# Right-hand steps of the first down layer placed beside the first half of each row pair only, one block of the weight combinations kept in another buffer, one warm-up matmul less

## The chip, the cores and the metric

The kernel runs on one core of one Trainium2 chip. The metric is the device time of one execution in microseconds (us), as the median of several runs. The kernel before took 1056.25 us (three runs, 1054.87 to 1056.70).

## The reference

The program is one attention layer with a sigmoid in place of the softmax, followed by two feed-forward blocks, all in float32:

```
scores = q @ k.T / sqrt(64) - log(448);  attn = sigmoid(scores);  x = attn @ v      (4 batches, 12 heads, 448 x 64)
xn = x / rms(x) * rms_g;   y = (silu(xn @ w_gate) * (xn @ w_val)) @ w_out             (1792 tokens, 768 -> 1536 -> 768)
h  = ((y @ w1) * (y @ w2)) @ w3;   out = h @ w_out2                                    (768 -> 1024 -> 1024 -> 768)
```

The kernel multiplies w3 by w_out2 first, so the second block ends with one product of h's 1024 features by a combined 1024 x 768 matrix. That product is called the down layer here.

## The kernel before, in words

Everything is computed transposed: features on the 128 partitions, 448 tokens (one batch) along the free axis. A product of float32 accuracy is made of three matmuls of a split number (high part by high part, low by high, high by low; `runs`, L339 to L347). Most layers use a Winograd form of the two-by-two block product: seven products of combined blocks in place of eight. The left-hand combinations (of the weights) are made by `Weights.winograd_blocks` (L164 to L183), the right-hand ones (of the activations) by `right_steps` (L569 to L638).

The four batches are worked in two pairs. For pair 0, then for pair 1, the last part of the program is an up layer (`c_winograd`, eight row blocks) and the down layer (`d_winograd`, L692 to L713, three row pairs n = 0, 1, 2). The first down layer is the one of pair 0. Each of its row pairs consists of two halves (e = 2n and e = 2n + 1), each half of seven parts, each part of six matmuls of 448 columns, which accumulate in the PSUM bank of that part: four banks of the tag `w` and three of the tag `m` (`psm`). In the second half the seven products come out one after the other, and `combine` (L715 to L745) takes each from PSUM: ScalarE copies product 0 to u (L721), and VectorE adds the others: product 1 to v (L724), then L728, L731, L734, two of L738 and L739, and L743. Until VectorE (or ScalarE) has read a bank, TensorE can't begin the same part of the next row pair.

Beside it runs a list of generators, `todo`; each call of `step` (L660) advances the first of them by one piece. In the first down layer they are: what is left of the combinations of the last h block (five steps); and for k = 0, 1, 2 `y_steps(k)` (L667), which prepare the right-hand blocks of the second pair's up layer. A `y_steps(k)` loads four tiles `ys` from DRAM (first step; the buffers of the tag `held` are four, so each load waits until the tile that had the buffer is no longer read), does nothing for one step, and begins with its third: two subtractions t1 and t2 from `ys` (the second needs the fourth tile) and the first of seven `put`s. A put lets ScalarE copy the high part, and VectorE subtract it for the low part in the step after (`low`, L587). A `y_steps` takes ten steps; the one of k = 2 takes `wait` more, since its last four puts go to buffers that the down layer itself reads until its last row pair. All these VectorE instructions have line L575 and are pinned behind the instruction that was traced before them on VectorE (`keep_in_program_order`); the others are ordered by the planner, which simulates the program with estimated costs and issues an engine's ready instruction that was traced first.

The weights come as four quarters a11, a12, a21, a22 in one tile `wd`; `winograd_blocks` makes two sums and a difference (L171 to L173), yields six blocks, and makes the seventh, a12 - s2, at L179. Each yielded block is copied for its high part by ScalarE (L134), and GpSimd subtracts that for the low part (L138). L179 writes the seventh over a12, which was the third block.

At the start, eight matmuls of a tile of ones (L81 and L82, `WARM`) run on TensorE while the first inputs arrive; each is two matmul instructions in the trace.

Of the kernel before, what the change touches and what calls it, by code (L numbers as in the profile page):

```python
# [13 lines left out]
ALU = mybir.AluOpType  # L14
# [19 lines left out]
AHEAD_B1 = (2, 2, 2, 0, 0, 0)  # L34
AHEAD_B2 = (2, 2, 2, 1, 1, 0)
WH = 3 * P
WARM = 8
STEP = 8


# [5 lines left out]
def fused_kernel(ctx: ExitStack, tc: tile.TileContext, qkv, wg, wv, wo, w1, w2, w3, wo2, gam, out):  # L46
    nc = tc.nc
# [32 lines left out]

    for _ in range(WARM):  # L81
        nc.tensor.matmul(ps_m.tile([P, 512], F32, tag="m", bufs=3, name="psm")[:, :P], ones, ones, start=True, stop=True)  # L82
# [5 lines left out]
    def scratch(name):  # L88
        return scr.tile([P, S], F32, tag="s", bufs=6, name=name)
# [4 lines left out]
    def psm():  # L94
        return ps_m.tile([P, 512], F32, tag="m", bufs=3, name="psm")
# [44 lines left out]
    class Weights:  # L140
# [23 lines left out]
        def winograd_blocks(self):  # L164

            while True:
                f, w, keep = self.loaded.pop(0)
                a11, a12, a21, a22 = (f[:, j, k * w : (k + 1) * w] for j in range(2) for k in range(2))
                s = wp.tile([P, WT], F32, tag="mag", bufs=1, name="s")
                s1, s2 = s[:, :w], s[:, w : 2 * w]  # L170
                nc.vector.tensor_tensor(out=s1, in0=a21, in1=a22, op=ALU.add)  # L171
                nc.vector.tensor_tensor(out=s2, in0=s1, in1=a11, op=ALU.subtract)  # L172
                nc.vector.tensor_tensor(out=a21, in0=a11, in1=a21, op=ALU.subtract)  # L173
                if keep is not None:
                    nc.sync.dma_start(out=keep[0], in_=s2)
                    nc.sync.dma_start(out=keep[1], in_=a21)
                    nc.sync.dma_start(out=keep[2], in_=s1)
                yield from (a11, s2, a12, a21, a22, s1)
                nc.vector.tensor_tensor(out=a12, in0=a12, in1=s2, op=ALU.subtract)  # L179
                if keep is not None:  # L180
                    nc.sync.dma_start(out=keep[3], in_=a12)
                self.out -= 1
                yield a12  # L183

        def make_blocks(self):

# [152 lines left out]
    def runs(ps, wtile, kw, xts, first, last):  # L339

        n = len(xts)
        for r, (wi, xi) in enumerate(RUNS):
            for j, xt in enumerate(xts):
                w = wtile[:, wi, (kw + j) * P : (kw + j + 1) * P]
                nc.tensor.matmul(  # L345
                    ps, w, xt[:, xi, :], start=first and r == 0 and j == 0, stop=last and r == 2 and j == n - 1
                )  # L347
# [211 lines left out]
    def right_tile(name, bl):  # L559
        p, n, step = {0: (r1a, 6, STEP), 1: (r1b, 6, 0), 2: (pools["xw"], 9, STEP)}[bl]  # L560
        return parts(p, f"x{bl}", n, name, step=step)

    def ab_tile(name, n):

        if n < 2 * KF1:
            return h_tile(name, n // 2)
        return right_tile(name, (n - 2 * KF1) // 2)

    def right_steps(k, b, home=None, down=False, wait=None):  # L569

        def sub(out, in0, in1, op=ALU.subtract):
            i = nc.vector.tensor_tensor(out=out, in0=in0, in1=in1, op=op)  # L575
            if down or wait is not None:
                tc.keep_in_program_order(i)

        late = []

        def put(j, bl, src):
            t = acts["d" if down else "w", j, k] = ab_tile(f"w{j}", 7 * k + j) if down else right_tile(f"w{j}", bl)
            nc.scalar.activation(t[:, 0, :], src, AF.Copy)
            low()
            late.append((t, src))

        def low():  # L587
            if late:
                t, src = late.pop()
                sub(t[:, 1, :], src, t[:, 0, :])  # L590

        if wait is None:
            put(0, 0, b[0])
            yield
            t1 = home()
            sub(t1, b[1], b[0])
            put(5, 1, t1)
            yield
            while len(b) < 4:
                low()  # L600
                yield
            put(2, 0, b[2])
            yield
            t3 = home()
            sub(t3, b[3], b[1])
            put(3, 2, t3)
            yield
            t2 = home()
            sub(t2, t3, b[0], ALU.add)
            put(1, 2, t2)  # L610
            yield
            t4 = home()
            sub(t4, b[2], t2)
            put(4, 2, t4)
            yield
            put(6, 1, b[3])
            yield
            low()
            return
        t1 = scratch("t1")  # L620
        sub(t1, b[1], b[0])
        t2 = scratch("t2")
        sub(t2, b[3], t1)
        put(1, 2, t2)
        yield
        sub(b[1], b[3], b[1])
        put(3, 2, b[1])
        yield
        sub(t2, b[2], t2)
        put(4, 2, t2)  # L630
        yield
        for _ in range(wait):
            low()
            yield
        for j, bl, x in ((0, 0, b[0]), (2, 0, b[2]), (5, 1, t1), (6, 1, b[3])):
            put(j, bl, x)
            yield
        low()  # L638
# [7 lines left out]
    def load_y(g, k):  # L646
        y = []
        for m in (k, k + 3):
            for b in range(2):
                y.append(held("ys"))  # L650
                nc.sync.dma_start(out=y[-1], in_=yd.pop((g, b, m)))
        return y
# [7 lines left out]
    def step():  # L660

        if todo:
            next(todo[0], None)
            if inspect.getgeneratorstate(todo[0]) == inspect.GEN_CLOSED:
                todo.pop(0)

    def y_steps(k):  # L667
        y = load_y(1, k)
        for _ in range(2):
            yield  # L670
        yield from right_steps(k, y, wait=5 if k == 2 else 0)

    def product_bank():
        return psm()[:, :S]
# [1 line left out]
    def bank():  # L676
        return ps_w.tile([P, 512], F32, tag="w", bufs=4, name="w")[:, :S]
# [14 lines left out]
    def d_winograd(g, first, n):  # L692

        ps = [bank() if j < 4 else psm()[:, :S] for j in range(7)]

        def part(e, j):
            i, c = divmod(7 * e + j, 3)
            t = W.get(first + i)[:, :, c * 2 * P : (c + 1) * 2 * P]
            h = D_HALVES[e][1]
            runs(ps[j], t, 0, [acts["d", j, 2 * h + k] for k in range(2)], e == 2 * n, e > 2 * n)  # L700
            W.split_to(first + i + 3)
            W.load_to(first + i + 6)
            return ps[j]

        def done(b, *rows):
            for j, o in enumerate(rows):
                m = 2 * n + j
                nc.sync.dma_start(out=out[m * P : (m + 1) * P, (2 * g + b) * S : (2 * g + b + 1) * S], in_=o)

        for j in range(7):  # L710
            part(2 * n, j)
            step()
        combine(lambda j: part(2 * n + 1, j), done)  # L713

    def combine(product, done, home=None):  # L715

        tt = nc.vector.tensor_tensor

        u, v, c21 = (scratch(n) for n in ("u", "v", "c21"))
        p1 = product(0)  # L720
        nc.scalar.activation(u, p1, AF.Copy)  # L721
        step()
        p6 = product(1)
        tt(out=v, in0=p6, in1=u, op=ALU.add)  # L724
        step()
        p2 = product(2)
        c11 = home() if home else scratch("c11")
        tt(out=c11, in0=p2, in1=u, op=ALU.add)  # L728
        step()
        p7 = product(3)  # L730
        tt(out=u, in0=p7, in1=v, op=ALU.add)  # L731
        step()
        p4 = product(4)
        tt(out=c21, in0=p4, in1=u, op=ALU.add)  # L734
        done(0, c11, c21)
        step()
        p5 = product(5)
        tt(out=u, in0=p5, in1=u, op=ALU.add)  # L738
        tt(out=v, in0=p5, in1=v, op=ALU.add)  # L739
        step()  # L740
        p3 = product(6)
        c12 = home() if home else v
        tt(out=c12, in0=p3, in1=v, op=ALU.add)  # L743
        done(1, c12, u)
        step()  # L745

    def a_winograd(m):
        def done(b, g, v):
# [146 lines left out]
    steps = []  # L895
# [18 lines left out]
    beside = a[half_a:] + b[:5]  # L914
# [45 lines left out]
    for m in range(KF2):  # L960
        c_winograd(i_c, m)
    todo.extend(y_steps(k) for k in range(KD // 2))
    for n in range(KD // 2):
        d_winograd(0, i_d, n)
# [3 lines left out]
    for n in range(KD // 2):  # L968
        d_winograd(1, i_d2, n)
# [59 lines left out]
```

## Time and profile before

| quantity | value |
|---|---|
| median of three runs | 1056.25 us |
| the profiled execution's own time | 1054.65 us |
| its span, first to last instruction | 1052.7 us |
| TensorE busy | 1044.4 us, 99% |
| VectorE busy | 811.8 us, 77% |
| ScalarE busy | 441.6 us, 42% |
| GpSimd busy | 394.7 us, 37% |
| DMA traffic | 164.26 MB, mean 156 GB/s |

The span lies 1.95 us below the execution's own time; that rest lies before the first and behind the last instruction. Busy shares are averages over the whole span: stages differ, and in the stretch of the first down layer (about 841 to 895 us) VectorE is busy nearly all the time. PE is TensorE's matmuls, PEld its weight loads, DVE VectorE, ACT ScalarE, POOL GpSimd, SP the queue that issues most DMAs. Matmuls overlap each other, so the distance from one start to the next is what a matmul costs, and a busy PE says less than a late start.

### The profile page before, as it was taken

What the parts mean: (1) busy time and instruction counts of PE and PEld (TensorE: products, weight loads), DVE (VectorE), ACT (ScalarE), POOL (GpSimd) and SP (SyncE); (2) the same over time, 40 slices, a digit from 0 to 9 for tenths busy, and PEclk for the clock granted to TensorE, in tenths of its full rate; (3) what the DMA queues carried; (4) which work ended last, traced back from release to release, by engine and by line L of the source; (5) the groups of instructions that cost most, each with busy time, mean ns of one, the idle gap of its engine ahead of it and who ended that gap; (6) DMA issues with size and microseconds to landing.
All of it is one profiled execution on the core that took longest, in us unless ns stands there. A gap on an engine that the chain in (4) does not pass through costs nothing. (4 is left out here: it accounts for less than half of the span.)

```text
span 1052.7 us, 14293 instructions
## 1 busy us (share of the span) xinstructions
PE 1044.4 (99%) x5146; PEld 889.5 (84%) x5146; DVE 811.8 (77%) x1172; ACT 441.6 (42%) x800; POOL 394.7 (37%) x342
## 2 busy tenths in 40 slices
PE   9999999999999999999999999999999999999998
PEld 4338799998777878799999999999999998999997
DVE  5998988878575788697777779973688999777754
ACT  5684332222554653344444444332344355343431
POOL 2646400000212222103555553223555667555562
PEclk9999999999999999999999999999999999999999
DMA  7653555666444677763221113867333345433131
GB/s 261 237 195 103 162 183 182 209 236 222 146 147 150 190 239 267 249 224 101 76 70 63 62 61 105 281 216 253 129 121 120 100 131 151 156 114 112 51 96 70
DMA packets 72934, 164.26 MB, mean 156 GB/s; under 512 B 7200, under 2 KB 45216, under 8 KB 72864
## 3 DMA queue, kind: packets, MB, share of 16 engines
q1 hardware_dynamic: 70560, 160.20, 46.3%
q10 hardware_dynamic: 2304, 3.15, 0.8%
q8 instruction: 41, 0.67, 0.3%
q14 instruction: 29, 0.24, 0.1%
HBM read 119.67 MB, written 43.65 MB: 155 GB/s over the span
## 5 line engine op out<-in xcount | busy, mean ns | idle before, releaser
L345 PE MATMUL w<-w,ws 128*128 128x448 f32 x2052 | 420.4, 366 | 1.6 <-DVE v L724 1.6
L345 PEld LDWEIGHTS w<-w,ws 128*128 128x128 f32 x2052 | 385.1, 188 | 34.8 <-DVE v L724 1.9
L138 POOL TENSOR_TENSOR ws<-wd,ws 128x384 fp32r<-128x384 f32 (+1 forms) x160 | 155.3, 986 | 158.0 <-ACT ws L134 109.6
L345 PE MATMUL psm<-hm,ws 128*128 128x448 f32 x864 | 178.0, 367 | 0.0
L345 PEld LDWEIGHTS psm<-hm,ws 128*128 128x128 f32 x864 | 161.9, 188 | 15.8 <-issue 2.0
L345 PE MATMUL psm<-x,ws 128*128 128x448 f32 x648 | 136.8, 369 | 0.4 <-DVE s L793 0.4
L345 PEld LDWEIGHTS psm<-x,ws 128*128 128x128 f32 x648 | 120.9, 188 | 15.2 <-issue 3.5
L138 POOL TENSOR_TENSOR ws<-wf,ws 128x768 fp32r<-128x768 f32 (+1 forms) x51 | 92.4, 1813 | 101.3 <-ACT ws L134 100.2
L134 ACT ACTIVATE ws<-wf 128x768 fp32r<-128x768 f32 (+1 forms) x81 | 66.5, 825 | 100.6 <-PE psm L345 23.0
L134 ACT ACTIVATE ws<-wd 128x384 fp32r<-128x384 f32 (+1 forms) x160 | 70.9, 475 | 68.0 <-PE w L345 47.9
L427 POOL TENSOR_TENSOR qk<-qk 128x960 fp32r<-128x960 f32 x10 | 23.7, 2370 | 175.2 <-ACT qk L426 175.2
L114 DVE TENSOR_SCALAR mag<-wd 128x768 uint32<-128x768 uint32 (+1 forms) x76 | 46.6, 613 | 44.8 <-DMA wd<-in_wo 17.3
L138 POOL TENSOR_TENSOR ws<-s,ws 128x384 fp32r<-128x384 f32 (+1 forms) x64 | 63.2, 987 | 47.3 <-ACT ws L134 43.9
L124 DVE SCALAR_TENSOR_TENSOR wf<-wd,wf 128x768 uint32<-128x768 uint32 (+1 forms) x76 | 78.6, 1034 | 2.2
L127 DVE SCALAR_TENSOR_TENSOR wf<-wd,wf 128x768 uint32<-128x768 uint32 (+1 forms) x76 | 76.3, 1005 | 1.1
L345 PEld LDWEIGHTS psm<-o,ws 128*128 128x128 f32 x384 | 67.3, 188 | 2.4 <-issue 1.6
L345 PE MATMUL psm<-o,ws 128*128 128x384 f32 x384 | 69.3, 339 | 0.0
L116 DVE TENSOR_SCALAR wf<-mag 128x768 uint32<-128x768 uint32 (+1 forms) x76 | 55.6, 731 | 16.7 <-POOL ws L138 11.5
L508 POOL TENSOR_TENSOR acc<-acc,sq 128x448 f32<-128x448 f32 x20 | 27.3, 1364 | 94.3 <-ACT sq L507 94.3
L115 DVE TENSOR_SCALAR mag<-mag 128x768 f32<-128x768 f32 (+1 forms) x76 | 51.7, 681 | 1.7
L179 DVE TENSOR_TENSOR wd<-wd,s 128x384 f32<-128x384 f32 (+1 forms) x32 | 26.5, 829 | 33.8 <-POOL ws L138 33.8
L171 DVE TENSOR_TENSOR s<-wd 128x384 f32<-128x384 f32 (+1 forms) x32 | 27.7, 865 | 29.5 <-POOL ws L138 29.3
(122 smaller groups left out, 1293.3 us busy)
## 6 DMA issues: line engine op xcount, KB each, us to landing
wd<-in_wo SPq DMA_DIRECT2D x20, 768.0 KB, 5.4
wd<-in_w SPq DMA_DIRECT2D x16, 768.0 KB, 5.2
wd<-in_wg SPq DMA_DIRECT2D x12, 768.0 KB, 4.5
wd<-in_wv SPq DMA_DIRECT2D x12, 768.0 KB, 5.5
raw<-in_qkv SPq DMA_DIRECT2D x12, 736.0 KB, 4.2
wd<-in_w SPq DMA_DIRECT2D x16, 512.0 KB, 4.5
w<-wf SPq DMA_DIRECT2D x16, 384.0 KB, 2.6
wd<-w SPq DMA_DIRECT2D x16, 384.0 KB, 3.8
```

The source lines that it names most:

```text
L114: nc.vector.tensor_scalar(out=mag.bitcast(U32), in0=hi, scalar1=0x7FFFFFFF, scalar2=None, op0=ALU.bitwise_and)
L115: nc.vector.tensor_scalar(out=mag, in0=mag, scalar1=HI_MIN, scalar2=HI_MAX, op0=ALU.max, op1=ALU.min)
L116: nc.vector.tensor_scalar(out=u, in0=mag.bitcast(U32), scalar1=3, scalar2=0x3FFFFFFF, op0=ALU.logical_shift_left, op1=ALU.bitwise_and,)
L124: nc.vector.scalar_tensor_tensor(out=u, in0=hi, scalar=0xC0000000, in1=u, op0=ALU.bitwise_and, op1=ALU.bitwise_or)
L127: nc.vector.scalar_tensor_tensor(out=u, in0=lo, scalar=29, in1=u, op0=ALU.logical_shift_right, op1=ALU.bitwise_or)
L134: nc.scalar.activation(t[:, 0, :w], f[:, :w], AF.Copy)
L138: lows.tensor_tensor(out=t[:, 1, :w], in0=f[:, :w], in1=t[:, 0, :w], op=ALU.subtract)
L171: nc.vector.tensor_tensor(out=s1, in0=a21, in1=a22, op=ALU.add)
L179: nc.vector.tensor_tensor(out=a12, in0=a12, in1=s2, op=ALU.subtract)
L345: nc.tensor.matmul(ps, w, xt[:, xi, :], start=first and r == 0 and j == 0, stop=last and r == 2 and j == n - 1)
L427: nc.gpsimd.tensor_tensor(out=lo, in0=x, in1=hi, op=ALU.subtract)
L508: nc.gpsimd.tensor_tensor(out=acc[b], in0=acc[b], in1=sq, op=ALU.add)
```

## The change

Three edits. `WARM` is 7 in place of 8. L179 and what follows it write the seventh block over a11 (the first block) in place of a12 (the third). And in the down layer the first half of row pairs 0 and 1 calls `step` twice behind each part, while their second half calls it not at all (all seven `step()` of `combine` become `beside()`); row pair 2 keeps one step behind each part of both halves. The wait of `y_steps(2)` is four steps in place of five. `combine` as the up layers and the gated layer call it keeps its steps (the argument's default).

```
-WARM = 8
+WARM = 7
...
-                nc.vector.tensor_tensor(out=a12, in0=a12, in1=s2, op=ALU.subtract)
+                nc.vector.tensor_tensor(out=a11, in0=a12, in1=s2, op=ALU.subtract)
                 if keep is not None:
-                    nc.sync.dma_start(out=keep[3], in_=a12)
+                    nc.sync.dma_start(out=keep[3], in_=a11)
                 self.out -= 1
-                yield a12
+                yield a11
...
-        yield from right_steps(k, y, wait=5 if k == 2 else 0)
+        yield from right_steps(k, y, wait=4 if k == 2 else 0)
...
         for j in range(7):
             part(2 * n, j)
             step()
-        combine(lambda j: part(2 * n + 1, j), done)
+            if n < 2:
+                step()
+        combine(lambda j: part(2 * n + 1, j), done, None, n == 2)
 
-    def combine(product, done, home=None):
+    def combine(product, done, home=None, steps=True):
 
         tt = nc.vector.tensor_tensor
+        beside = step if steps else lambda: None
...
-        step()
+        beside()
```

## Rows read from the trace of the kernel before

**Rows 1.** Page, part 1: busy time, share of the span, instructions by engine.

```profile
PE 1044.4 (99%) x5146; PEld 889.5 (84%) x5146; DVE 811.8 (77%) x1172; ACT 441.6 (42%) x800; POOL 394.7 (37%) x342
```

**Rows 2.** Busy time by stretch: e = 3, then the first half of n = 2 (e = 4).

```profile
866.74:875.28 8.54, 8.54 (x43) 7.88 (x42) 8.38 (x12) 5.83 (x14) 5.58 (x7) 1.00 0.40 119
875.28:886.32 11.04, 9.22 (x44) 7.57 (x42) 10.56 (x20) 2.13 (x7) 7.16 (x8) 1.00 0.70 211
```

**Rows 3.** Timeline of PE: start, us, what, count, and idle time before with its releaser.

```profile
866.74 5.04 PE L345 MATMUL w<-w,ws 128*128 128x448 f32 x24
871.62 3.82 PE L345 MATMUL psm<-w,ws 128*128 128x448 f32 x18
875.28 1.40 PE L345 MATMUL w<-w,ws 128*128 128x448 f32 x6
878.24 3.96 PE L345 MATMUL w<-w,ws 128*128 128x448 f32 x18 [1.56 <-DVE v L724]
882.46 4.02 PE L345 MATMUL psm<-w,ws 128*128 128x448 f32 x18 [0.26 <-DVE c L734]
886.32 5.05 PE L345 MATMUL w<-w,ws 128*128 128x448 f32 x24
```

**Rows 4.** Timeline of DVE in the first down layer.

```profile
849.17 0.95 DVE L171 TENSOR_TENSOR s<-wd 128x256 f32<-128x256 f32 x1 [0.63 <-POOL ws L138]
...
853.20 0.94 DVE L179 TENSOR_TENSOR wd<-wd,s 128x256 f32<-128x256 f32 x1 [0.80 <-POOL ws L138]
854.06 0.61 DVE L575 TENSOR_TENSOR t<-ys 128x448 f32<-128x448 f32 x1
...
867.92 0.41 DVE L179 TENSOR_TENSOR wd<-wd,s 128x256 f32<-128x256 f32 x1
...
875.43 1.16 DVE L575 TENSOR_TENSOR w<-t,w 128x448 fp32r<-128x448 f32 x1
876.51 1.14 DVE L575 TENSOR_TENSOR w<-ys,w 128x448 fp32r<-128x448 f32 x1
877.58 0.61 DVE L724 TENSOR_TENSOR v<-w,u 128x448 f32<-128x448 f32 x1
878.11 0.61 DVE L575 TENSOR_TENSOR w<-ys,w 128x448 fp32r<-128x448 f32 x1
878.64 0.61 DVE L728 TENSOR_TENSOR c<-w,u 128x448 f32<-128x448 f32 x1
879.18 0.62 DVE L575 TENSOR_TENSOR w<-t,w 128x448 fp32r<-128x448 f32 x1
...
881.26 0.61 DVE L575 TENSOR_TENSOR w<-ys,w 128x448 fp32r<-128x448 f32 x1
881.79 0.61 DVE L734 TENSOR_TENSOR c<-psm,u 128x448 f32<-128x448 f32 x1
...
884.60 0.62 DVE L575 TENSOR_TENSOR t<-ys 128x448 f32<-128x448 f32 x1
```

**Rows 5.** Timeline of POOL around the late L724.

```profile
876.07 1.10 POOL L138 TENSOR_TENSOR ws<-s,ws 128x256 fp32r<-128x256 f32 x1
877.13 2.18 POOL L138 TENSOR_TENSOR ws<-wd,ws 128x256 fp32r<-128x256 f32 x2
```

**Rows 6.** Source line L651, 800 to 900 us: the loads of ys from issue to landing.

```profile
DMA to landing us min/median/max: 2.4/3.1/4.8
```

**Rows 7.** Timeline of the first 10 us.

```profile
2.59 0.43 SPq L420 DMA_DIRECT2D raw<-in_qkv  x1
...
4.20 0.64 PE L82 MATMUL psm<-ones 128*128 128x128 f32 x2
...
4.77 1.09 PE L441 MATMUL sc<-raw 64*128 64x448 f32 x2
...
9.38 0.99 PE L441 MATMUL psm<-raw 128*128 128x448 f32 x2 [0.69 <-ACT a L459]
```

**Rows 8.** DMA issues of 0 to 3 us: KB each, us to landing.

```profile
raw<-in_qkv SPq DMA_DIRECT2D x1, 736.0 KB, 6.6
```

**Rows 9.** Source line L179, 300 to 1000 us: what DVE waited for before it.

```profile
  POOL ws L138: 28.3, 22
```

More of the change, by code (lines that the diff above doesn't have):

```diff
@@ L721, in combine @@
         nc.scalar.activation(u, p1, AF.Copy)
-        step()
+        beside()
         p6 = product(1)
         tt(out=v, in0=p6, in1=u, op=ALU.add)
-        step()
+        beside()
         p2 = product(2)
@@ L728, in combine @@
         tt(out=c11, in0=p2, in1=u, op=ALU.add)
-        step()
+        beside()
         p7 = product(3)
         tt(out=u, in0=p7, in1=v, op=ALU.add)
-        step()
+        beside()
         p4 = product(4)
@@ L735, in combine @@
         done(0, c11, c21)
-        step()
+        beside()
         p5 = product(5)
@@ L739, in combine @@
         tt(out=v, in0=p5, in1=v, op=ALU.add)
-        step()
+        beside()
         p3 = product(6)
@@ L744, in combine @@
         done(1, c12, u)
-        step()
+        beside()
     def a_winograd(m):
```

## The prediction, made before the changed kernel ran

> **What bounds the kernel now.** I read the busy shares first: TensorE is busy 99% of the span [rows 1], so the kernel ends when TensorE's queue ends, and an edit counts only where TensorE starts a matmul late or where it has fewer of them. VectorE at 77% can't be the bound on average, but it can be one in a stage. Next I cut the first down layer into its halves. The fourth half takes 8.54 us, the fifth, which has the same 42 matmuls, 11.04 us [rows 2]: 2.50 us are lost there, with VectorE busy 10.56 of the 11.04. The PE timeline says where. Twenty-four matmuls start 4.88 us apart in all (866.74 to 871.62), 0.203 us each. The fifth half's first six start at 875.28, so the seventh was due at 876.50; it started at 878.24, 1.74 us late, for L724 of row pair 1. Eighteen matmuls later 881.90 was due and 882.46 came, 0.56 us late, for L734; the remaining 0.20 us (886.12 due, 886.32 came) has no such releaser [rows 3]. The DVE timeline shows why L724 was late: VectorE worked without a gap and had low parts of L575 in front of it, until 877.58, though the product that L724 reads was finished twelve matmuls into the half before, near 869.2 [rows 3, 4]. So VectorE was some 8 us behind TensorE. The change acts on that backlog. All that can be won here is about 2.5 us of 1056, or 0.24%.
>
> **Part 1: the steps move.** Nothing is added or removed: the same subtractions, puts and loads are issued; one idle wait step of `y_steps(2)` goes, which issues nothing. The places: five steps left from the h block, then ten, ten and fourteen, on 14 + 14 + 14 places. Row pair 0's first half now takes the five and the first nine of k = 0; row pair 1's first half takes the tenth of k = 0, all ten of k = 1 and the first three of k = 2. Before, row pair 1's second half had steps seven to ten of k = 1 and the first three of k = 2 between its combine instructions.
>
> For L724 of row pair 1 this works in both directions. In front of it come three more low parts, those that stood behind it: 878.11, 879.18 and 881.26. They took 0.53, 0.54 and 0.53 us to the next instruction [rows 4]: 1.60 us. Alone and behind each other, while GpSimd subtracts, the lows of 875.43 and 876.51 took 1.08 and 1.07 us [rows 4, 5]: then 3.2 us. I take 1.60, these instructions' own rows, and keep 3.2 as the end. Out of the way go two idle times of VectorE earlier in the layer, since its chain has no gap from there to 877.58: 0.80 us in front of L179 at 853.20 (part 2), and 0.63 us at 849.17, which the last lows of the h block fill, being traced in front of it now [rows 4]. So L724 starts at 877.58 + 1.60 - 1.43 = 877.75, with the end at 879.35; below, if none of the moved lows delays it, 876.15. TensorE goes on 0.66 us behind L724's start, as before (877.58 to 878.24), so its seventh matmul comes at 878.41: 1.91 us late, with ends of 0.3 and 3.5.
>
> L724 of row pair 0 has all of k = 0 in front of it too. They began at 854.06, behind the 0.80 us that goes, so from 853.3 ten subtractions at 0.54 us end at 858.7, just in time for the seventh matmul of row pair 1 (its first half starts some 8.6 us before 866.74, and 1.22 us later that matmul is due, at 859.4); at 1.08 us each they would end at 864. But what TensorE loses there it doesn't lose again at row pair 2, where the same VectorE chain is late: the loss at 876.50 is the total, so I add nothing.
>
> Behind L724 there are no right-hand steps any more; L728 to L743 follow each other, and the 0.56 us at L734 should go. What is late next is the start of k = 2. Its first three steps are traced in front of that combine; t2 needs the fourth `ys`, whose buffer is only free when the last low of k = 1 is done, and a load takes 2.4 to 4.8 us, 3.1 in the median, to land [rows 6]. Before, t1 of k = 2 came at 884.60, behind the whole combine [rows 4]. Since the planner fills VectorE's waits with other ready work (it put L179 and L171 to L173 there at k = 1), I expect L724 and perhaps L728 to be ordered in front of t2, and some later combine instruction behind it: 0 to 1.5 us, I take 0.4. The loads are issued by SP past the four stores of row pair 0's output; they land beside matmuls and are covered, except for that t2. New sum of this half's loss: 1.91 + 0.40 + 0.20 = 2.51 us, against 2.50 before. The wait moves, and nothing is won.
>
> In row pair 2 the puts come one place earlier behind the half that last reads their buffers; I price this at nothing, with the matmuls of the fifth and sixth half (2 x 8.5 us) as the cover; without it, one low part of 0.54 us.
>
> **Part 2: the seventh block over a11.** L179 writes where both readers are long done, and so no longer waits for GpSimd's read of a12. VectorE waited 28.3 us, 22 times, in front of L179 over the later layers [rows 9]; but of that only the 0.80 us counted above lies in a stage where TensorE waits for VectorE. Elsewhere it is hidden by TensorE's own queue. Beside GpSimd's read it could take 0.94 us, as at 853.20, in place of the 0.41 at 867.92 [rows 4], half a microsecond each; I take nothing.
>
> **Part 3: one warm-up less.** A warm-up is two matmul instructions of 0.21 us (4.20 to 4.77 holds two and a short gap), so the first score product can start at about 4.34 in place of 4.77 [rows 7]: 0.43 us. But the score product at 9.38 reads the second pair's inputs, whose load was issued at 2.59 and landed 6.6 us later, at 9.2 [rows 7, 8]. So the transfer takes the place of the wait, and 0.1 us is left, at most 0.43 if that landing comes earlier. No row shows TensorE with a shorter warm-up; the first two score matmuls last 1.09 us together [rows 7], and if a later pair became as slow, that would cost no more than what the edit can bring. I take 0.1 won, with ends of 0.4 won and 0.4 lost.
>
> **The sum.** 2.51 - 2.50 - 0.10 is -0.1 us. The profiled execution took 1054.65 us (span 1052.7 and 1.95 around it), so it would take 1054.55. That execution lies 1.6 us under the median of the runs shown; the same step from the median gives 1056.25 - 0.1, say 1056.2 us.
>
> **The rivals.**
> 1. The waits go. If the planner orders the combine of row pair 1 in front of the moved lows, or VectorE's chain is 2 us quicker without the mixture, TensorE meets no late bank: 2.3 to 2.5 us and 0.1 to 0.4 at the start, 1053.6 us. For it: VectorE's combine instructions read PSUM and never show the long 1.1 us form (0.61 in all of [rows 4]). Against it: the backlog of 8 us is there already, and the lows go in front.
> 2. The load in front of L724: slower. If t2 of k = 2 is ordered in front of L724, it waits for a load that can't start before the last low of k = 1 ends, at 877.75 to 879.35. Plus 3.1 us to land and 0.54 for t2, L724 starts at 881.4 to 883.0, and the seventh matmul is 5.5 to 7.2 us late in place of 1.74; with 0.56 saved at L734, 3.2 to 4.9 us more: 1059.4 to 1061.1 us. It decides from the point where VectorE has no other work ready between the last low of k = 1 and that landing.
> 3. GpSimd slows the moved steps. Subtractions behind each other between two SBUF tiles take the 1.08 us form beside GpSimd: the 3.2 us end above, 1.6 more than I took, and 0.5 for t1: 1058.3 us. The Trainium skill ("SBUF — State Buffer", section "Who interferes with whom") says that a VectorE instruction with two SBUF inputs contends with a GpSimd instruction that reads SBUF, while one with at most one SBUF input doesn't. By that rule the change packs the contending instructions together in the first halves. The rows agree in part: 876.51 was long beside GpSimd's 876.07, but 878.11 took 0.53 us beside GpSimd's 877.13 [rows 4, 5].
> 4. It doesn't do what it says: VectorE is so far behind that its order hardly changes, and only the start differs: 1056.1 us.
>
> **How the numbers follow.** Chances: the forecast 0.42, rival 1 0.25, rival 2 0.15, rival 3 0.10, rival 4 0.08. A measurement of this kernel can't tell less than 0.2%, 2.1 us, from no change. The forecast and rival 4 lie inside of that, rival 1 outside (2.6), rival 3 on its edge, half to each side: faster 0.25, same 0.55, slower 0.20. The forecast's own range, by the ends of its terms (0.3 to 3.5, 0 to 1.5, 0.4 to either side), is 1054.3 to 1058.7; to leave out no more than 2 in 10, I take 1053.4 to 1059.4, which holds rival 1 and cuts rival 2.
>
> **What would show it.** Right: in the changed trace the seventh matmul of the third row pair waits 1 to 3 us for L724, VectorE has no gap in the layer's middle, L179 has no wait on GpSimd, and the score product near 9.3 us waits for its load. Step wrong: the fifth half takes 8.6 us (rival 1), or over 13 us with t of L575 waiting for `ys` just in front of L724 (rival 2); low parts of 1.1 us throughout (rival 3). The prediction falls if a stage that TensorE filled before shows late matmuls for another reason.

## The result, and the profile after

The changed kernel takes 1062.14 us (median of six runs, 1061.32 to 1063.38), the kernel before 1056.27 (six runs): ratio 1.0061, 95% interval 1.0048 to 1.0074. It is slower by 5.9 us, clear of the 0.2% bound, and 2.7 us above the stated range. The profiled execution took 1062.23 us with a span of 1060.0, which is 7.3 us more than the span before; that execution of the kernel before was one of its faster ones, so the medians differ by less.

Where do the 7.3 us arise? I followed the same places of the program (a norm, the start of a layer) along TensorE's time in both traces. At 346 us (the third norm, line L514) the changed kernel is 1.24 us ahead (346.36 against 347.60). Six us later it is 0.5 us behind (the wait at 352.40, below), and stays so until the second half of the first down layer (850.07 against 849.57). From there to the first matmul of the up layer it takes 52.05 us in place of 45.30: 6.75 us more. Behind that the difference stays.

The first down layer by stretches, the two that answer to [rows 2]: the fourth half, and the fifth (first half of the third row pair). Columns: window, us, busy us of PE, PEld, DVE, ACT, POOL (with counts), TensorE's granted clock (1.00 is full speed), DMA share, GB/s.

```profile
867.65:876.20 8.55, 8.55 (x43) 7.69 (x41) 5.98 (x10) 3.96 (x10) 4.63 (x6) 1.00 0.29 88
876.20:893.58 17.38, 12.70 (x44) 10.78 (x44) 14.42 (x24) 8.59 (x21) 11.13 (x13) 0.71 0.43 136
```

The fifth half takes 17.38 us where 42 matmuls at 0.203 us need 8.54, and VectorE, with 5.98 of 8.55 us, is no longer always busy in the fourth. Its PE timeline, against [rows 3]:

```profile
858.58 2.61 PE L345 MATMUL w<-w,ws 128*128 128x448 f32 x12
861.41 2.72 PE L345 MATMUL w<-w,ws 128*128 128x448 f32 x12 [0.22 <-DVE c L731]
...
872.54 3.82 PE L345 MATMUL psm<-w,ws 128*128 128x448 f32 x18
878.84 2.58 PE L345 MATMUL w<-w,ws 128*128 128x448 f32 x6 [2.48 <-ACT u L724]
883.62 6.44 PE L345 MATMUL w<-w,ws 128*128 128x448 f32 x18 [2.20 <-DVE v L727]
889.90 3.84 PE L345 MATMUL psm<-w,ws 128*128 128x448 f32 x18
893.58 5.05 PE L345 MATMUL w<-w,ws 128*128 128x448 f32 x24
```

(The lines have moved by three: L724 is now ScalarE's copy u, which was L721, and L727 VectorE's v, which was L724.) Eighteen matmuls after 872.54 the next was due at 876.20; it came at 878.84, 2.64 us late, and for ScalarE, not VectorE. At full speed the seventh was then due at 880.06 and came at 883.62. And the eighteen from there took 6.28 us to the next start in place of 3.66. Another 0.39 us goes at 861.41 (due 861.02). The sum closes: the seventh matmul is 6.20 us late against its place in an unbroken row (877.42), where it was 1.74 late; 0.76 us of smaller delays are gone; 2.62 us go to the slow eighteen and 0.39 to the last one named: 6.71 of the 6.75. The slow matmuls are the clock (columns: window, us, busy PE, granted clock, DMA share, GB/s):

```profile
876.00:878.00 2.00, 0.36 (x2) 1.00 0.23 52
878.00:880.00 2.00, 1.16 (x3) 0.72 0.83 277
882.00:884.00 2.00, 0.38 (x1) 0.50 0.00 0
886.00:888.00 2.00, 2.00 (x7) 0.50 0.76 238
890.00:892.00 2.00, 2.00 (x12) 1.00 0.34 129
```

After a stand of 2.64 us (a stand is a time in which TensorE has matmuls left and starts none) TensorE resumes and the granted clock goes to 0.50, the 1.2 GHz level; at 890 it is back at 1.00 (2.4 GHz), within the run of matmuls that began at 883.62. In the kernel before, the stand of 1.74 us [rows 3] left it at 1.00 [rows 2].

Why are u and v late? VectorE first, against [rows 4] (start, us, what, idle time before it and its releaser):

```profile
865.83 0.62 DVE L575 TENSOR_TENSOR t<-ys 128x448 f32<-128x448 f32 x1
870.15 0.94 DVE L171 TENSOR_TENSOR s<-wd 128x256 f32<-128x256 f32 x1 [3.70 <-POOL ws L138]
...
878.05 1.15 DVE L575 TENSOR_TENSOR w<-ys,w 128x448 fp32r<-128x448 f32 x1
880.18 0.78 DVE L575 TENSOR_TENSOR t<-ys 128x448 f32<-128x448 f32 x1 [0.98 <-DMA ys<-y]
882.07 0.63 DVE L575 TENSOR_TENSOR t<-ys,t 128x448 f32<-128x448 f32 x1 [1.11 <-DMA ys<-y]
882.62 0.42 DVE L171 TENSOR_TENSOR s<-wd 128x256 f32<-128x256 f32 x1
882.95 0.62 DVE L727 TENSOR_TENSOR v<-w,u 128x448 f32<-128x448 f32 x1
```

Two things stand out. The last low of k = 1 (878.05) is followed by t1 and t2 of k = 2, which wait 0.98 and 1.11 us for their loads, and L727 comes behind them, 5.4 us later than its counterpart at 877.58 (4.9 when the layer's later start is taken off). And between t1 of k = 1 and L171 VectorE stands for 3.70 us, for GpSimd. Followed back, that wait is again a load, through ScalarE and GpSimd:

```profile
867.03 0.58 ACT L583 ACTIVATE w<-ys 128x448 fp32r<-128x448 f32 x1 [4.00 <-DMA ys<-y]
867.51 0.71 ACT L134 ACTIVATE ws<-wd 128x256 fp32r<-128x256 f32 x2
...
876.56 0.58 ACT L583 ACTIVATE w<-t 128x448 fp32r<-128x448 f32 x1 [0.48 <-DVE t L575]
877.04 1.01 ACT L134 ACTIVATE ws<-wd 128x256 fp32r<-128x256 f32 x3
877.96 0.40 ACT L134 ACTIVATE ws<-s 128x256 fp32r<-128x256 f32 x1
878.27 0.52 ACT L724 ACTIVATE u<-w 128x448 f32<-128x448 f32 x1
```

```profile
867.99 1.43 POOL L138 TENSOR_TENSOR ws<-wd,ws 128x256 fp32r<-128x256 f32 x2 [3.96 <-ACT ws L134]
869.38 0.74 POOL L138 TENSOR_TENSOR ws<-s,ws 128x256 fp32r<-128x256 f32 x1
```

ScalarE's copy of a `ys` tile of k = 1 (the third one, whose load was issued at 862.35), which nothing pins, stands 4.00 us at the head of its queue for that load; the weight copies (L134) wait behind it, GpSimd behind those, and VectorE's L171 behind GpSimd, which still reads the one buffer of s. And u, whose product was finished near 868.9, stands in ScalarE's queue behind all the copies of k = 1, which follow the late VectorE, and behind four copies of weights.

The loss around 350 us lies ahead of the layer. VectorE and GpSimd there, first the kernel before, then the changed one:

```profile
349.05 0.56 DVE L114 TENSOR_SCALAR mag<-wd 128x768 uint32<-128x768 uint32 x1 [3.54 <-DMA wd<-in_w]
349.78 2.55 POOL L427 TENSOR_TENSOR qk<-qk 128x960 fp32r<-128x960 f32 x1 [5.09 <-ACT qk L426]
```

```profile
348.54 2.26 POOL L427 TENSOR_TENSOR qk<-qk 128x960 fp32r<-128x960 f32 x1 [5.09 <-ACT qk L426]
348.67 2.54 DVE L114 TENSOR_SCALAR mag<-wd 128x768 uint32<-128x768 uint32 x1 [4.40 <-DMA wd<-in_w]
```

The compute queues run 1.24 us ahead, the load of the weights only 0.38. So L114, which starts when its load lands, now starts behind GpSimd's L427 and not ahead of it, and takes 2.54 us in place of 0.56; L796 behind it frees a PSUM bank late, and TensorE's weight load at 352.40 waits 1.85 us. The Trainium skill ("SBUF — State Buffer", section "Who interferes with whom") says that an elementwise instruction of this kind can take the port pair which VectorE shares with GpSimd, and that the one that starts first keeps it to its end; the trace agrees, since L114 ends 0.41 us behind L427. (The prediction's short form, by which one SBUF input doesn't contend, leaves out such instructions: L114 reads one tile and waited.) In the kernel before an instruction beside L427 is long too, L364 at 350.65 with 2.16 us (0.62 in the changed kernel), but it comes behind the one which frees the bank.

This wait is not shown to come from the warm-up edit. All nine traces with seven warm-ups have it (0.88 to 1.48 us; in some it is L115, the next instruction, that is long), but so have two of the five with eight: e4 (1.08 us) and e11 (1.47 us). And the 0.5 us is less than the traces differ when the layer's second half begins (848.83 to 852.36 us at full clock).

### The profile page after: what moved, and what is told of

It is laid out like the page before. It is cut to its first block, busy times and chain, and to the rows that moved or that the text cites. A ratio compares the mean times of both kernels' runs of the same rounds, so it can differ in the third digit from the quotient of the medians.

```text
span 1060.0 us, 14291 instructions
## 1 busy us (share of the span) xinstructions
PE 1047.6 (99%) x5144; PEld 891.8 (84%) x5144; DVE 807.4 (76%) x1172; ACT 443.6 (42%) x800; POOL 390.6 (37%) x342
## 4 chain that ended last, share of the span: by engine, by line
PE 91%; DVE 3%; DMA 2%; POOL 1%; issue 1%; ACT 1%; SPq 0%; DVEq 0%; POOLq 0%; ACTq 0%
PE psm L345 37%; PE w L345 37%; PE av L474 5%; PE psa L345 4%; PE sc L441 3%; PE psm L441 3%; PE av L470 2%; POOL ws L138 1%; DVE w L575 1%; DMA wd<-in_w 1%; DMA raw<-in_qkv 1%; DMA out_t<-u 0%; DMA ys<-y 0%; POOL qk L427 0%; DVE mag L114 0%
## 5 line engine op out<-in xcount | busy, mean ns | idle before, releaser
L134 ACT ACTIVATE ws<-wf 128x768 fp32r<-128x768 f32 (+1 forms) x81 | 66.6, 825 | 95.9 <-PE psm L345 24.6
L134 ACT ACTIVATE ws<-wd 128x384 fp32r<-128x384 f32 (+1 forms) x160 | 71.1, 476 | 68.0 <-PE w L345 50.4
L427 POOL TENSOR_TENSOR qk<-qk 128x960 fp32r<-128x960 f32 x10 | 23.4, 2341 | 177.2 <-ACT qk L426 177.2
L114 DVE TENSOR_SCALAR mag<-wd 128x768 uint32<-128x768 uint32 (+1 forms) x76 | 46.2, 608 | 47.6 <-DMA wd<-in_wo 16.7
L116 DVE TENSOR_SCALAR wf<-mag 128x768 uint32<-128x768 uint32 (+1 forms) x76 | 58.2, 766 | 15.2 <-POOL ws L138 10.0
L171 DVE TENSOR_TENSOR s<-wd 128x384 f32<-128x384 f32 (+1 forms) x32 | 26.5, 828 | 43.1 <-POOL ws L138 43.0
L115 DVE TENSOR_SCALAR mag<-mag 128x768 f32<-128x768 f32 (+1 forms) x76 | 52.8, 695 | 1.7
L461 ACT ACTIVATE a<-sc,bias_s 128x896 f32<-128x896 f32 x48 | 45.4, 995 | 7.2 <-PE sc L441 7.1
```

What stands on the lines that cost most here:

```text
L114: nc.vector.tensor_scalar(out=mag.bitcast(U32), in0=hi, scalar1=0x7FFFFFFF, scalar2=None, op0=ALU.bitwise_and)
L115: nc.vector.tensor_scalar(out=mag, in0=mag, scalar1=HI_MIN, scalar2=HI_MAX, op0=ALU.max, op1=ALU.min)
L116: nc.vector.tensor_scalar(out=u, in0=mag.bitcast(U32), scalar1=3, scalar2=0x3FFFFFFF, op0=ALU.logical_shift_left, op1=ALU.bitwise_and,)
L134: nc.scalar.activation(t[:, 0, :w], f[:, :w], AF.Copy)
L461: nc.scalar.activation(a, both, **sigmoid)
```

## The experiments

All were timed against the kernel before. The column "layer" is the time from the second half of the first down layer to the up layer's first matmul in the profiled execution (before: 45.30 us; changed kernel: 52.05); it is one execution each.

| run | median us | before us | ratio, 95% | layer us |
|---|---|---|---|---|
| e1 warm-up edit alone | 1054.96 | 1055.22 | 0.9998 (0.9989 to 1.0007) | 45.43 |
| e2 block edit alone | 1053.65 | 1055.22 | 0.9986 (0.9977 to 0.9995) | 43.70 |
| e3 moved steps alone | 1062.30 | 1055.22 | 1.0068 (1.0055 to 1.0081) | 53.24 |
| e4 steps and block | 1061.11 | 1055.22 | 1.0055 (1.0042 to 1.0069) | 51.97 |
| e5 k = 2 later | 1058.69 | 1055.44 | 1.0034 (1.0022 to 1.0046) | 47.62 |
| e6 row pair 0 only | 1056.36 | 1055.44 | 1.0011 (1.0002 to 1.0021) | 46.54 |
| e7 row pair 1 only | 1059.96 | 1055.72 | 1.0046 (1.0030 to 1.0061) | 49.84 |
| e8 no loads for k = 1, 2 | 1056.28 | 1055.44 | 1.0009 (0.9999 to 1.0019) | 45.95 |
| e9 24 matmuls in the stands | 1060.30 | 1055.44 | 1.0045 (1.0033 to 1.0058) | 49.69 |
| e10 copies pinned | 1060.97 | 1055.72 | 1.0059 (1.0043 to 1.0075) | not compared |
| e11 block edit, copies pinned | 1054.31 | 1055.72 | 0.9989 (0.9980 to 0.9998) | 44.48 |
| e12 k = 2 later, copies pinned | 1055.83 | 1055.82 | 1.0004 (0.9990 to 1.0018) | 44.96 |

**e1 to e4: which edit.** Each edit of the change made alone in the kernel before, and the last two together (the changed kernel with `WARM = 8`). In each text the theory is what I held, the rival what else could be.

> Only the warm-up edit: WARM 7, the rest as before. Theory A (the early gain is given back in front of the third norm): the trace runs 1.2 us ahead of the kernel before at 346 us, then the first decode instruction L114 near 348.7 starts behind GpSimd's L427 in place of ahead of it and takes some 2.5 us in place of 0.56, TensorE waits near 350 us for L793 for about 1.5 us, and the time is 0 to 1 us over the kernel before: 1056.3 to 1057.3. Rival (the edit costs or gains by itself, with no give-back): the early gain stays to the end, 1055.0 us; or all 0.5 us and more of the loss ahead of the down layer has another cause and the time is that of before.

> Only the seventh block over a11. Theory: L179 stops waiting for GpSimd (28 us of VectorE waits go) and the time stays within 1 us of the kernel before, 1055.5 to 1056.8, since TensorE waits for none of it outside the first down layer. Rival: L179 beside GpSimd's reads slows the lows and TensorE's waits grow in the first down layer: 1057.5 us or more.

> Only the moved steps (with the wait of four). Theory: they alone make the loss in the first down layer, about 6.6 us: three late matmuls in the third row pair's first half and the granted clock at 0.5 for some 10 us behind; 1061.5 to 1063 us. Rival (only the combination is slow, each edit alone is not): under 1058 us and no stretch with a granted clock of 0.5.

> The changed kernel with eight warm-ups. Theory: the loss in the down layer stays, 1061 to 1063 us, and it differs from the moved steps alone by under 1 us. Rival (the warm-up edit is what shifts the planner's order in the down layer): it is back at 1056 to 1057 us.

The moved steps alone make the whole loss, and a little more; e4 lies 1.2 us under e3, with intervals that overlap. The warm-up edit alone is worth nothing that can be measured. Its median is near the rival's figure, but so is the kernel before in the same runs; its trace decides, with a lead of 1.75 us at the third norm (345.85) and none behind it (355.66 against 355.67). L114 and L427 there:

```profile
348.09 2.62 DVE L114 TENSOR_SCALAR mag<-wd 128x768 uint32<-128x768 uint32 x1 [4.34 <-DMA wd<-in_w]
348.03 2.26 POOL L427 TENSOR_TENSOR qk<-qk 128x960 fp32r<-128x960 f32 x1 [5.09 <-ACT qk L426]
```

The block edit alone is faster, by 0.05 to 0.23%: 1.5 us, more than its theory allowed. Its third row pair, PE and then VectorE:

```profile
874.48 5.24 PE L345 MATMUL w<-w,ws 128*128 128x448 f32 x24
879.97 4.18 PE L345 MATMUL psm<-w,ws 128*128 128x448 f32 x18 [0.25 <-DVE c L734]
```

```profile
874.53 0.61 DVE L724 TENSOR_TENSOR v<-w,u 128x448 f32<-128x448 f32 x1
```

L724 comes at 874.53, 3 us earlier than in [rows 4] (0.74 us of it because the layer starts earlier), and the wait of 1.56 us for it is gone; 0.6 us at L734 are left. So it beats both kernels. It doesn't end all waits of L179 on GpSimd, as its theory had it: over the whole span 17.9 us in 14 waits are left of 33.8 in 24, presumably since a11's reader can be late too.

**e5, e6, e7: which steps.** In e5 the line `if n < 2:` of the changed kernel becomes `if n == 0 or n == 1 and j < 4:`. In e6 and e7 only one row pair is doubled (the diff is that of e6; e7 has `n == 1` in the first added line and `n != 1` in the second):

```
-            if n < 2:
+            if n == 0:
                 step()
-        combine(lambda j: part(2 * n + 1, j), done, None, n == 2)
+        combine(lambda j: part(2 * n + 1, j), done, None, n > 0)
```

> The changed kernel, but row pair 1 doubles the steps beside its first four parts only, so that the three first steps of k = 2 (the loads, t1, t2) come in row pair 2. Theory A (the load of k = 2 in front of the combine of row pair 1 is what makes TensorE late at its third row pair): L727 of row pair 1 starts some 4 us earlier, near 879, the late seventh matmul shrinks from 2.2 to under 1 us, TensorE doesn't fall to the clock of 0.5, and the time falls by 4 to 6 us against the changed kernel, to 1056.5 to 1058.5. Rival B (the backlog of VectorE and ScalarE from the steps of k = 1, with the 3.7 us gap, makes it): the wait of TensorE for ScalarE's copy u stays at 2 us or more, the clock falls all the same, and the time stays over 1060.

> The changed kernel with the steps doubled in row pair 0 only; row pairs 1 and 2 have one step behind each part of both halves, as before. Theory: the harm is in row pair 1, where the steps of k = 1 and the loads of k = 2 come in front of its combine; with that undone the third row pair's waits are those of the kernel before or less, no clock of 0.5, 1054 to 1057 us. Rival (the harm begins in row pair 0, by the late loads of k = 1 and the gap behind t1 of k = 1): the gap stays, TensorE is late at the third row pair by 3 us or more, 1059 us or more.

> The changed kernel with the steps doubled in row pair 1 only; row pairs 0 and 2 have one step behind each part of both halves, as before. Theory (the larger part of the loss is made by row pair 1, by the loads of k = 2 in front of its combine, and is there whatever row pair 0 does): t2 of k = 2 waits for its load in front of L727 of row pair 1, the clock falls to 0.5, 1059 to 1062 us. Rival (it takes both row pairs, since only the later start of k = 1 in row pair 0 brings the gap): under 1058 us and no stretch at 0.5.

e5 decided for neither side alone. L727 came at 879.38, as theory A had it, and TensorE no longer waited for it; but u stayed late, 2.00 us, with VectorE's gap at 3.36 us as before, and the clock fell after that stand (0.50 from 880 to 882):

```profile
879.38 0.61 DVE L727 TENSOR_TENSOR v<-w,u 128x448 f32<-128x448 f32 x1
878.79 6.90 PE L345 MATMUL w<-w,ws 128*128 128x448 f32 x24 [1.84 <-ACT u L724]
```

The 24 matmuls take 6.74 us to the next start in place of 4.88. The median, 3.2 us over the kernel before, lies between both forecasts. e6 agrees with its theory in time and clock: the gap is there (3.69 us), but it costs only 0.9 us, with waits of 1.29 us for u and 0.71 us for L734 and no fall of the clock. The waits are not "those of the kernel before or less": the fifth half takes 11.85 us (875.01 to 886.86) against 11.04. e7 agrees too: L727 comes at 881.42, behind t1, t2 and the three lows, and TensorE stands. VectorE shows no gap there, but t2 does wait for its load: it was issued at 878.25, as the last low was done, landed 2.5 us later, and t2 starts at 880.88; t1 and L171 to L179 fill the time:

```profile
881.42 0.62 DVE L727 TENSOR_TENSOR v<-w,u 128x448 f32<-128x448 f32 x1
877.33 1.49 PE L345 MATMUL w<-w,ws 128*128 128x448 f32 x6 [1.28 <-ACT u L724]
882.09 5.94 PE L345 MATMUL w<-w,ws 128*128 128x448 f32 x18 [3.27 <-DVE v L727]
```

So each row pair's doubling brings a wait of its own, and row pair 1's costs by far more (4.2 us against 0.9).

**e8: loads or work.** `y_steps` of k = 1 and 2 take the tiles that k = 0 loaded.

```
+    kept_y = []
...
-        y = load_y(1, k)
+        if k == 0:
+            kept_y[:] = load_y(1, k)
+        y = kept_y
```

> The changed kernel, but k = 1 and k = 2 work on the four tiles of k = 0 and load nothing (left out: their eight loads; every subtraction and copy stays in its place, the second pair's up layer gets wrong blocks). Theory A (waits for loads at the head of ScalarE's and VectorE's queues): the gap of 3.7 us of VectorE and the wait in front of t2 go, TensorE waits under 1 us in the down layer, no clock of 0.5, 1053.5 to 1056 us. Rival B (it is the amount of VectorE work in front of L727, loads or not): VectorE is busy without a gap, L727 of row pair 1 still comes after 879, and the time stays over 1059 us.

All moved subtractions and copies are there, and of the 0.61% over the kernel before 0.52% are gone (1.0009 against 1.0061); the layer falls from 52.05 to 45.95 us, and the clock stays at 1.00. L731 (v in that kernel) comes at 878.10. Theory A holds in the main: with the eight loads left out the loss is all but gone. (This run takes away the transfers along with the waits for them; e12, below, keeps all loads and changes only the order.) It said under 1 us of waits, though, and there are more:

```profile
878.77 2.72 PE L345 MATMUL w<-w,ws 128*128 128x448 f32 x12 [0.53 <-DVE v L731]
882.95 1.50 PE L345 MATMUL w<-w,ws 128*128 128x448 f32 x6 [1.46 <-DVE u L738]
```

**e9: the clock.** Matmuls that nobody reads, in the two stands of row pair 2's first half.

```
+FILL = (12, 12)
...
+            if g == 0 and n == 2 and j in (0, 1):
+                idle = ps_av.tile([P, 512], F32, tag="av", bufs=1, name="idle")[:, :S]
+                x = acts["d", 0, 0]
+                for r in range(FILL[j]):
+                    tc.keep_in_program_order(
+                        nc.tensor.matmul(idle, x[:, 0, :P], x[:, 0, :], start=True, stop=True)
+                    )
             part(2 * n, j)
```

> The changed kernel with 12 matmuls added in front of the first and 12 in front of the second part of row pair 2's first half (their result is read by nobody; 12 take 2.4 us at the full clock), where TensorE stands 2.5 and 2.2 us. Theory (some 3.8 of the 6.6 us lost are the clock that falls while TensorE stands, not the waits): the granted clock stays at 1.00, the added matmuls lie in the waits, and the time falls by 3 to 4 us, to 1058 to 1059.5, in spite of 24 more matmuls. Rival (the clock doesn't matter much, or falls for another reason): 1062 us or, with the added matmuls on the path, up to 1067.

With 24 matmuls more the layer is 2.36 us shorter, and the clock stays at 1.00:

```profile
876.00:880.00 4.00, 3.85 (x19) 1.00 0.64 179
880.00:884.00 4.00, 3.23 (x17) 1.00 0.15 50
```

The eighteen matmuls behind v take 3.89 us in place of 6.28. The gain is smaller than expected, since the slow first six lay in the wait for v anyway; that wait's end doesn't move (33.58 us behind the start of the layer's second half, against 33.55), as it hangs on loads and VectorE. In the medians the gain is 1.8 us, 1.0045 against 1.0061, with intervals that overlap; the trace carries the price, 2.4 to 2.6 us for the clock. That the clock was kept shows in every execution: its mean over the span is 1.000 in the nine of e9 and 0.995 to 0.996 in the six of the changed kernel.

**e10, e11, e12: ScalarE's early copy.** In `put`, for the `y_steps` alone:

```
-            nc.scalar.activation(t[:, 0, :], src, AF.Copy)
+            i = nc.scalar.activation(t[:, 0, :], src, AF.Copy)
+            if wait is not None:
+                tc.keep_in_program_order(i)
```

> The changed kernel with ScalarE's high-part copies of the y_steps pinned behind what was traced before them on ScalarE, so that the copy of the first ys tile of k = 1 no longer stands, waiting for its load, in front of the copies of weights (L134). Theory (the 3.7 us gap of VectorE is that chain: load, ScalarE's early copy, L134, GpSimd's L138, VectorE's L171): the gap is under 1 us, ScalarE's wait for ys in front of the weights goes, and the time falls by 2 to 4 us against the changed kernel, 1057.5 to 1060. Rival (VectorE's own wait for the fourth tile makes the gap): VectorE waits as long, now in front of t2, and the time stays at 1061 or more.

> The kernel before with the seventh block over a11 and the y_steps' ScalarE copies pinned; no moved steps, eight warm-ups. Theory: what is left of TensorE's waits in the first down layer behind that edit alone is 0.25 us, so pinning can bring no more than that: 1053.2 to 1054.0 us. Rival: the pinned copies stand later in ScalarE's queue, the lows of VectorE wait for them, and L724 is late again: 1055 us or more.

> The changed kernel with both remedies: row pair 1 doubles the steps beside four parts only (k = 2 starts in row pair 2), and ScalarE's copies of the y_steps are pinned. Theory (two chains of waits for loads make the loss: k = 1's through ScalarE's early copy and GpSimd to VectorE's L171, k = 2's through t2 to L727): both go, TensorE's waits in the down layer come to under 1.5 us, the granted clock stays at 1.00, and the time is within 1 us of the kernel before's: 1054.5 to 1056.5. Rival (the sheer number of steps ahead of the combine of row pair 1 is enough): TensorE waits 2 us or more for L727 or u, 1057.5 us or more.

e10 has its mechanism right and its price wrong. The gap of 3.70 us becomes 1.14 us in front of t2, TensorE's wait for u falls to 0.72 us, but the time is that of the changed kernel within the intervals (1.0059 against 1.0061). The next wait took its place: TensorE now stands 3.73 us for v, which is still behind t1 and t2 of k = 2:

```profile
881.62 1.51 PE L345 MATMUL w<-w,ws 128*128 128x448 f32 x6 [0.72 <-ACT u L726]
886.86 5.44 PE L345 MATMUL w<-w,ws 128*128 128x448 f32 x18 [3.73 <-DVE v L729]
```

This profiled execution (1064.14 us) ran at a granted clock of 0.95 from end to end, so its layer isn't compared; the three others took 1060.13 to 1061.21 us, 1 to 2 us under the changed kernel and over what was expected. e12 takes away both waits, and the loss is gone, 1.0004 (its ten executions spread from 1053.08 to 1060.83), with the steps still doubled in row pair 0 and beside four parts of row pair 1:

```profile
877.86 2.73 PE L345 MATMUL w<-w,ws 128*128 128x448 f32 x12 [0.35 <-DVE v L729]
881.33 1.50 PE L345 MATMUL w<-w,ws 128*128 128x448 f32 x6 [0.74 <-DVE u L736]
```

e11 adds the pinning to the block edit alone: 0.9989 against 0.9986, no further gain (layer 44.48 us against 43.70), as its theory said, if 0.3 us over the stated figures.

## Why the prediction was wrong

**The step that failed** is in part 1: "I expect L724 and perhaps L728 to be ordered in front of t2, and some later combine instruction behind it". The planner put t1 and t2 of k = 2, and L171, in front of v (L727 here), and t1 and t2 waited for loads: the part taken at 0.4 us became most of the seventh matmul's 6.20 us (in e5, without it, TensorE is 2.00 us late, for u). That is rival 2, to which I gave 0.15; it said 5.5 to 7.2 us late and 1059.4 to 1061.1 us in all, and had the wait right and the time 1 us short (1062.14). With the steps of k = 2 behind the combine, e5 takes back about half of the loss (1.0061 to 1.0034), and the rest is the second chain's: with that pinned, the same move takes back nearly all of it (e10 to e12, 1.0059 to 1.0004).

**What rival 2 lacked** is a term of the sum, the granted clock: these stands of TensorE weren't paid once, because the matmuls behind them ran at 0.50; the prediction had the clock nowhere in its sum (2.4 to 2.6 us, e9). It also lacked ScalarE: I priced VectorE's queue and named SP's, but u is ScalarE's, and it was 2.64 us late behind the copies that the moved steps issue; before, no wait of TensorE in this layer named ScalarE. In the changed kernel this adds nothing to the sum by itself, since v is later still; it comes to light in e5, where v is early and TensorE waits for u.

**"VectorE has no gap in the layer's middle"** was wrong, with 3.70 us. The unpinned copy of a `ys` tile rode ahead of the weight copies and held ScalarE, GpSimd and VectorE up in turn. I counted the moved step's loads as covered "except for that t2", and didn't ask which other queue had a reader of them at its head. By itself this gap is cheap (e6); it counts together with the later wait. And of the 1.43 us that were to go out of VectorE's way, 0.63 stayed: L171 at 847.99 waits that long for GpSimd as before.

**The three moved lows** were taken at 0.54 us; with GpSimd beside them the last two took 0.62 and 1.15 us, and in e7 the last three (874.05, 876.01, 877.08) 1.14 to 1.16. That is rival 3's size, and it is the smaller matter here: in e8 the work is all there and the layer costs 0.65 us more than before.

**Row pair 0**: I added nothing for its L724; 0.39 us went at 861.41, for L731 (L728 before the change) and not for it.

**The seventh block**: the mechanism was right in the first down layer, and 0.80 us was its term; measured alone it is 1.5 us (0.5 to 2.4), as the wait for L724 of row pair 1 goes altogether. That L179 has no wait on GpSimd any more was wrong: 17.3 us in 13 waits are left in the changed kernel. Beside the moved steps it still shows: with it their layer is 51.97 us (e4), without it 53.24 (e3), where TensorE waits 1.92 us for L731 in row pair 0 and not 0.21.

**The warm-up**: 0.1 us net agrees with what was measured (0.2 us less, with an interval of 1.2 less to 0.7 more), but by luck. The first score product starts at 4.34, as worked out, and the load of the second pair does take the wait's place:

```profile
8.43 0.99 PE L441 MATMUL psm<-raw 128*128 128x448 f32 x2 [0.26 <-DMA raw<-in_qkv]
```

But it landed earlier than before, after 5.7 us in place of 6.6, which isn't the edit's doing each time (in e8, with seven warm-ups too, that product starts at 9.41). So the trace ran up to 1.24 us ahead, and the loss at 350 us was nowhere in the prediction.

**The range**: the ends named for it add up to about 1053.9 to 1059.3 us, not 1054.3 to 1058.7; the measured time lies above either.

## What to carry to other kernels

When a step is moved forward, follow every reader of its loads on every engine, and ask what stands behind that reader in the queue: here it was neither the amount of work nor its own engine, but a load's wait in front of the instructions that free PSUM banks. Don't price a stand of TensorE by its length alone; look whether the matmuls behind it still run at the same clock. And take an edit of several parts apart first: one of these three was a gain, hidden behind a loss more than four times as large (7.1 us, e3).

## What the runs showed of the hardware that was not expected

A wait of TensorE can be paid a second time in its clock: behind waits of 1.56 us (before), 1.29 us (e6) and 1.46 us (e8) the granted clock stayed at 1.00; behind 1.84 us (e5) and 2.48 us (changed kernel) it went to 0.50, and the matmuls of the changed kernel ran at half speed until 889. The length of the one wait doesn't decide it, though. In e3 the clock stayed at 1.00 behind 1.92 us, and behind 2.30 us as well (the six matmuls took 1.49 us), and fell only in the stand that followed these six. TensorE's rows, and then window, us, busy PE, granted clock, DMA share, GB/s:

```profile
861.89 2.71 PE L345 MATMUL w<-w,ws 128*128 128x448 f32 x12 [1.92 <-DVE c L731]
879.12 1.49 PE L345 MATMUL w<-w,ws 128*128 128x448 f32 x6 [2.30 <-ACT u L724]
883.90 6.13 PE L345 MATMUL w<-w,ws 128*128 128x448 f32 x18 [3.29 <-DVE v L727]
```

```profile
880.00:882.00 2.00, 0.61 (x3) 0.98 0.55 159
882.00:884.00 2.00, 0.10 (x1) 0.50 0.00 0
```

The Trainium skill ("TensorE: Matmul & The Clock Gate", section "What's actually happening") says that the clock is set by how busy the array has been of late and has two levels; the 0.50 and 1.00 of these rows agree. The 0.95 of e10's profiled execution is neither, and no run here says where it comes from.

The port which VectorE and GpSimd share can turn a small shift into a long instruction: in e1 L114 started at 348.09, 0.06 us behind GpSimd's L427 (348.03), and took 2.62 us; in the kernel before it started ahead of L427 and took 0.56. L114 starts when the load of the weights lands, and how that falls against L427 differs between traces: in e4, with the eight warm-ups of the kernel before, L114 was ahead by 0.23 us and short, and L115 behind it took 2.51 us.
